# A wider look-ahead rule for the evacuating engine, together with a new scheduling table

## The chip, the cores and the metric

The kernel runs on one core of a Trainium2 chip. The metric is the device time of one execution in microseconds (us). The span of a profile is some 2.3 us shorter than its device time.

## The reference

It is one transformer layer on 2048 tokens of width 1024 in bf16. There are 32 query heads of width 32, but only one key head and one value head. The gated feed-forward part has width 3584.

```python
q = (x @ wq) as 32 heads;  k = x @ wk;  v = x @ wv          # k, v: one head of 32
p = softmax(q k^T * 32**-0.5);  attn = (p @ v) @ wo
h  = x + A(layernorm(x))                                    # A is the attention above
h2 = h + B(layernorm(h)),  B(x) = (sigmoid(x@w_gate) * (x@w_up)) @ w_down
```

## The kernel before

The program is a list scheduler. While the kernel is built, it simulates the engines with a table of assumed durations. It decides step by step what TensorE does next, and it fixes for each engine the order of its instructions. The built program holds these fixed orders, and its engines wait for each other at semaphores.

The spine is 512 "score visits". A visit is one block of eight row-tiled score matmuls, followed by two exponentials on ScalarE (`Pr`, 128x1024 each). Everything else on TensorE is filler between the visits: query projections, keys and values, probabilities times values (PV), output projections, feed-forward groups. If nothing can run, the scheduler puts in a matmul on the identity whose result nobody uses, called a dummy here.

In this program a finished PSUM bank is copied out ("evacuated") by ScalarE or VectorE: the query projections of 256 columns (`QTb`) took 384 to 478 ns on ScalarE and 418 to 425 ns on VectorE in before. This function chooses which of them does it:

```python
def evac(fn_act, fn_dve, n, deps, prio, dve_rate=0.96):
    now = pl.free["pe"]
    ready = now + 300.0 if v < 2 else 1e9
    a = max(pl.free["act"], now) + sum(o.occ for o in pl.heap["act"] if o.ready <= ready) + n / 1.2
    d = max(pl.free["dve"], now) + sum(o.occ for o in pl.heap["dve"] if o.ready <= ready) + n / dve_rate
    if a + (1000.0 * KNOBS[v // WIN][3] if v else 0.0) < d:
        return pl.op("act", fn_act, deps, prio=prio, **t_act(n))
    return pl.op("dve", fn_dve, deps, prio=prio, **t_dve(n, dve_rate))
```

`v` is the current visit. In visits 0 and 1 only those waiting operations count as backlog whose inputs will be there within 300 ns. Later all of them count (`1e9`).

`KNOBS` has 65 rows of eight small integers, one row for each eight visits (`WIN = 8`). They set thresholds and priorities. Entry 3 is an extra charge on ScalarE in us.

```python
pl.ahead = 100.0 * KNOBS[v // WIN][0] if v else 400.0
...
if can_s and run - t < 250.0 + 250.0 * KNOBS[v // WIN][4]:   # issue the next score visit now?
...
for cl in PRIO[KNOBS[v // WIN][2]]:                           # which filler class first
```

The first four x tiles are transposed on TensorE. The rest are transposed by DMA on the sync engine's queue, which also carries the stores of q and the weight loads:

```python
xT_ev[t] = dma(lambda: SP.dma_start_transpose(out=xnT4[t // 4][...], in_=x_sb[:, t, :]),
               f"xT{t}", ..., [xnorm[t]], prio=0, occ=1330.0)
...
q_store.append(dma(lambda: SP.dma_start(q_dram[:, g, tok:tok + n], qst[:, s, 0:n]), f"qs{s}", ..., [ev], prio=2))
```

The softmax here doesn't subtract the row's maximum and nothing guards it: scores larger than these inputs give would overflow.

## Time and profile before

| | before |
|---|---|
| device time | 1080.02 us, median of 3 (1079.95 to 1080.45) |
| span of the profiled run | 1078.0 us |
| last exponential ends | 1015.90 us |
| score matmuls of visit 3 start | 22.48 us |
| dummies in the front / later | 14 / 22 |

### The profile page before, as it was taken

The numbers are of one execution on the slowest core, as the hardware profiler recorded it, in microseconds if no ns is written. First come the engines' busy times: TensorE is split into PE (matmuls) and PEld (weight loads), VectorE is DVE, ScalarE is ACT, GpSimd is POOL, SyncE is SP. The second block draws the span as 40 slices with busy tenths as digits, with TensorE's granted clock in tenths as the row PEclk, the third lists the DMA queues.
The fourth block names the chain that finished last, engine by engine and source line by source line (L and its number), as shares of the span: only waits on it lengthen the run. The fifth ranks groups of instructions, "written<-read, shape, count | busy, mean of one in ns | idle before, by whom it ended". The sixth has DMA issues, their size and how long they took to land.

```text
span 1078.0 us, 31453 instructions
## 1 busy us (share of the span) xinstructions
PE 1043.5 (97%) x12925; PEld 489.3 (45%) x13094; DVE 903.2 (84%) x1736; ACT 1009.8 (94%) x1167; POOL 30.6 (3%) x58
## 2 busy tenths in 40 slices
PE   8999999999999999999999999999999999999999
PEld 7764434444444444444444444444444444444445
DVE  7899999898989879898888989898887988888721
ACT  6999999999999999999999999999999999999700
POOL 2100000000000000000000000000000000000000
PEclk9999999999999999999999999999999999999999
DMA  7997898929679695959879594955969489896994
GB/s 222 183 293 249 209 290 237 280 70 286 164 210 240 153 262 125 267 141 253 198 187 261 138 267 113 285 161 157 265 164 276 109 232 199 208 234 161 294 277 106
DMA packets 308623, 227.14 MB, mean 211 GB/s; under 512 B 119808, under 2 KB 299904, under 8 KB 308480
## 3 DMA queue, kind: packets, MB, share of 16 engines
q1 hardware_dynamic: 307296, 224.92, 81.8%
q8 instruction: 103, 1.69, 0.7%
q14 instruction: 40, 0.33, 0.1%
q10 hardware_dynamic: 1184, 0.20, 0.1%
HBM read 195.17 MB, written 7.86 MB: 188 GB/s over the span
## 4 chain that ended last, share of the span: by engine, by line
PE 73%; ACT 19%; issue 4%; DVE 2%; DMA 1%; SPq 0%; DVEq 0%
PE F_ps L415 57%; ACT Pr L707 18%; PE S_ps L415 16%; ACT tnh L1009 1%; DVE Ts L741 1%; DMA ring<-in_B_w_up_dram 1%; DVE Rc L806 0%; DMA ring<-in_A_x_dram 0%; DVE st L346 0%; DVE Oc L796 0%; DVE hact L291 0%; DVE st L348 0%; PE F_ps L444 0%; DVE Oc L291 0%; DVE Ts L748 0%
## 5 line engine op out<-in xcount | busy, mean ns | idle before, releaser
L707 ACT ACTIVATE Pr<-S_ps 128x1024 bf16<-128x1024 f32 x1024 | 968.9, 1156 | 3.3 <-PE S_ps L415 2.6
L741 DVE TENSOR_TENSOR Ts<-Ts,Pr 128x1024 bf16<-128x1024 bf16 x736 | 481.5, 677 | 33.7 <-ACT Pr L707 31.4
L415 PE MATMUL F_ps<-ring,hnT 128*128 128x512 bf16 (+1 forms) x1870 | 400.7, 380 | 13.1 <-issue 8.5
L415 PEld LDWEIGHTS F_ps<-ring,hnT 128*128 128x128 bf16 (+1 forms) x1957 | 147.6, 97 | 189.5 <-issue 48.3
L415 PE MATMUL S_ps<-QTb,kT 32*128 32x256 bf16 x4096 | 206.2, 273 | 1.2
L415 PE MATMUL F_ps<-zone,hact 128*128 128x512 bf16 (+2 forms) x1106 | 197.5, 377 | 9.5 <-issue 9.0
L415 PEld LDWEIGHTS S_ps<-QTb,kT 32*128 32x128 bf16 x4096 | 63.1, 92 | 206.3 <-ACT Pr L707 153.4
L415 PE MATMUL F_ps<-Pr,Vb 128*32 128x256 bf16 x4064 | 134.2, 274 | 0.3 <-issue 0.3
L415 PEld LDWEIGHTS F_ps<-zone,hact 128*128 128x128 bf16 (+1 forms) x1164 | 75.0, 97 | 83.5 <-issue 23.0
L415 PEld LDWEIGHTS F_ps<-Pr,Vb 128*32 128x32 bf16 x4064 | 96.8, 96 | 29.9 <-issue 17.0
L741 DVE TENSOR_TENSOR Ts<-Pr 128x1024 bf16<-128x1024 bf16 x128 | 86.6, 684 | 25.6 <-ACT Pr L707 25.1
L1013 DVE SCALAR_TENSOR_TENSOR hst<-tnh,F_ps 128x512 bf16<-128x512 f32 x107 | 73.3, 685 | 38.3 <-PE F_ps L415 36.4
L1009 ACT ACTIVATE tnh<-F_ps 128x512 f32<-128x512 f32 x105 | 77.5, 738 | 5.7 <-PE F_ps L415 5.7
L415 PE MATMUL F_ps<-zone 128*128 128x256 bf16 (+4 forms) x658 | 72.2, 272 | 2.3 <-issue 1.1
L415 PE MATMUL F_ps<-wo_sb,OT 128*128 128x512 bf16 (+1 forms) x283 | 58.4, 380 | 1.7 <-issue 1.6
L415 PEld LDWEIGHTS F_ps<-zone 128*128 128x128 bf16 (+1 forms) x667 | 43.1, 97 | 22.8 <-issue 7.4
L748 DVE TENSOR_TENSOR Ts<-Ts 128x1024 bf16<-128x1024 bf16 x64 | 43.9, 686 | 1.1
L358 POOL TENSOR_SCALAR zb<-mvb 128x1 bf16<-128x1 bf16 (+1 forms) x25 | 9.9, 397 | 993.6 <-DVE mvb L350 993.6
L1009 ACT ACTIVATE tnh<-S_ps 128x512 f32<-128x512 f32 x7 | 4.2, 597 | 35.3 <-PE S_ps L415 35.3
L291 DVE COPY Oc<-F_ps 128x256 f32<-128x256 f32 x60 | 25.3, 422 | 11.6 <-PE F_ps L415 10.7
L415 PEld LDWEIGHTS F_ps<-wo_sb,OT 128*128 128x128 bf16 (+1 forms) x294 | 21.0, 97 | 26.2 <-issue 6.8
L796 DVE TENSOR_TENSOR Oc<-F_ps,Oc 128x256 f32<-128x256 f32 x59 | 24.9, 423 | 7.5 <-PE F_ps L415 6.4
(84 smaller groups left out, 415.4 us busy)
## 6 DMA issues: line engine op xcount, KB each, us to landing
ring<-in_B_w_gate_dram SPq DMA_DIRECT2D x318, 256.0 KB, 4.8
ring<-in_B_w_up_dram SPq DMA_DIRECT2D x316, 256.0 KB, 4.6
zone<-in_B_w_down_dram SPq DMA_DIRECT2D x28, 256.0 KB, 3.7
h_sb<-in_A_x_dram SPq DMA_DIRECT2D x16, 256.0 KB, 4.5
out_dram<-h_sb SPq DMA_DIRECT2D x31, 128.0 KB, 3.0
ring<-in_A_x_dram SPq DMA_DIRECT2D x7, 512.0 KB, 5.3
QTb<-q_scratch SPq DMA_DIRECT2D x14, 256.0 KB, 5.4
Pr<-in_B_w_gate_dram SPq DMA_DIRECT2D x10, 256.0 KB, 4.1
```

What stands on the lines that cost most here:

```text
L291: lambda: DVE.tensor_copy(out=out_ap, in_=in_ap))
L358: f = pl.op("pool", lambda: POOL.tensor_scalar(out=zb[:, ph, sl].unsqueeze(2), in0=mvb[:, ph, sl, 1:2], scalar1=LN_EPS_BF16, scalar2=None, ...
L415: fn = lambda: PE.matmul(o, lhsT=l, rhs=r, start=start, stop=stop, **kw)
L707: exps[u] = pl.op("act", lambda slot=slot, pb=pb: ACT.activation(out=pslot(slot).rearrange("p (a b) -> p a b", a=2), in_=S_ps[:, pb:pb + 2 ...
L741: o = pl.op("dve", lambda T=T, a=a, b=b: DVE.tensor_tensor(out=T, in0=a, in1=b, op=ALU.add), deps, prio=4, **t_dve(1024, 1.92))
L748: merge_ev[G] = pl.op("dve", lambda T4=T4: DVE.tensor_tensor(out=T4[:, :, 0, :], in0=T4[:, :, 0, :], in1=T4[:, :, 1, :], op=ALU.add), [sum ...
L796: a = pl.op("dve", lambda: DVE.tensor_tensor(out=Oc[:, :], in0=O, in1=Ob, op=ALU.add), [last, oc_ev[G], o_ev.get(G - 1)], prio=0, **t_dve( ...
L1009: tanh_of[n] = pl.op("act", lambda: ACT.activation(out=tnh[:, :], in_=FB(b), func=ACTF.Tanh, scale=0.5), [last, tn_user.get(0)] + (tn_more ...
L1013: e = pl.op("dve", lambda: DVE.scalar_tensor_tensor(out=hst[:, n % NST, :], in0=tnh[:, :], scalar=1.0, in1=FB(b), op0=ALU.add, op1=ALU.mul ...
```

## The change

Its intent is that during visits 2 and 3 too, an operation that can't start yet should not count as a backlog. VectorE, waiting for a tile of x, would then get evacuations that ScalarE had to do between its exponentials.

```diff
-    KNOBS = [(4, 7, 0, 2, 2, 0, 0, 0), (0, 4, 0, 4, 1, 0, 0, 0), (2, 5, 0, 1, 3, 2, 1, 0), ... 62 more rows cut
+    KNOBS = [(4, 7, 1, 1, 2, 0, 0, 0), (0, 4, 1, 0, 2, 1, 0, 0), (2, 6, 0, 1, 2, 1, 1, 1), ... 62 more rows cut
...
-            ready = now + 300.0 if v < 2 else 1e9
+            ready = now + 300.0 if v < 4 else 1e9
```

More of the change, by code (lines that the diff above doesn't have):

```diff
@@ L170, in bass_sequential_preLN__grouped_kv_mqa__glu_gated_glu__prompt_kernel @@
     NCR = 12
-    KNOBS = [(4, 7, 0, 2, 2, 0, 0, 0), (0, 4, 0, 4, 1, 0, 0, 0), (2, 5, 0, 1, 3, 2, 1, 0), (3, 4, 1, 2, 3, 1, 1, 0), (3, 4, 0, 4, 2, 2, 1, 0), (1, 5, 1, 2, 3, 0, 1, 0), (4, 4, 0, 2, 2, 1, 0, 0), (4, 4, 1, 1, 3, 1, 1, 0), (1, 0, 0, 4, 3, 2, 0, 0), (3, 0, 1, 4, 2, 2, 0, 0), (1, 4, 1, 2, 3, 0, 1, 0), (4, 5, 0, 4, 2, 2, 0, 0), (3, 7, 0, 1, 3, 0, 0, 0), (2, 0, 1, 4, 2, 1, 0, 0), (3, 4, 0, 2, 2, 0, 1, 0), (2, 4, 0, 0, 3, 0, 1, 0), (3, 0, 0, 4, 3, 2, 0, 0), (2, 0, 0, 2, 3, 0, 1, 0), (0, 5, 0, 1, 3, 0, 0, 0), (1, 7, 1, 0, 3, 1, 0, 0), (0, 7, 0, 0, 3, 0, 1, 0), (2, 7, 0, 1, 3, 0, 0, 1), (4, 7, 0, 1, 3, 1, 1, 0), (1, 0, 1, 1, 3, 0, 0, 1), (4, 4, 0, 1, 3, 0, 0, 0), (3, 4, 1, 2, 3, 0, 1, 0), (2, 7, 0, 0, 3, 0, 1, 1), (0, 4, 1, 2, 2, 1, 1, 0), (3, 7, 1, 1, 2, 0, 1, 1), (4, 5, 0, 4, 3, 0, 0, 0), (4, 6, 0, 4, 3, 0, 0, 0), (2, 6, 1, 0, 3, 1, 1, 0), (1, 5, 1, 1, 2, 0, 1, 0), (4, 0, 0, 0, 2, 0, 0, 0), (4, 0, 0, 2, 3, 0, 1, 0), (2, 4, 0, 2, 2, 0, 1, 0), (0, 4, 0, 0, 3, 0, 0, 0), (3, 5, 0, 1, 2, 2, 0, 1), (1, 4, 0, 2, 2, 1, 1, 1), (4, 0, 0, 0, 3, 1, 0, 1), (1, 0, 0, 2, 3, 0, 0, 0), (2, 7, 0, 1, 3, 1, 0, 0), (3, 0, 0, 1, 2, 0, 0, 1), (1, 4, 0, 0, 3, 1, 1, 1), (0, 0, 1, 4, 2, 0, 0, 1), (3, 7, 0, 4, 3, 0, 0, 0), (1, 5, 1, 1, 2, 2, 0, 0), (4, 4, 0, 4, 2, 1, 1, 0), (0, 4, 0, 4, 3, 0, 1, 0), (1, 7, 0, 0, 2, 0, 1, 0), (1, 6, 0, 0, 3, 2, 1, 1), (2, 7, 0, 1, 3, 1, 0, 0), (4, 6, 1, 4, 2, 0, 0, 0), (0, 4, 0, 0, 2, 0, 0, 0), (4, 0, 0, 4, 3, 2, 1, 0), (3, 5, 1, 1, 3, 1, 0, 0), (2, 7, 0, 0, 3, 0, 0, 0), (3, 0, 0, 4, 2, 0, 1, 0), (4, 5, 0, 0, 3, 1, 0, 0), (4, 6, 0, 4, 1, 2, 0, 0), (4, 0, 0, 4, 3, 0, 0, 0), (4, 4, 0, 2, 2, 2, 0, 0), (4, 5, 0, 1, 1, 0, 1, 0), (4, 5, 1, 2, 2, 0, 0, 0), (2, 0, 0, 0, 2, 0, 0, 0)]
@@ new lines, in bass_sequential_preLN__grouped_kv_mqa__glu_gated_glu__prompt_kernel @@
+    KNOBS = [(4, 7, 1, 1, 2, 0, 0, 0), (0, 4, 1, 0, 2, 1, 0, 0), (2, 6, 0, 1, 2, 1, 1, 1), (2, 6, 1, 2, 2, 0, 0, 1), (0, 5, 1, 1, 3, 2, 1, 0), (3, 7, 1, 2, 3, 1, 1, 0), (0, 4, 0, 2, 2, 1, 0, 0), (3, 4, 1, 0, 3, 1, 1, 0), (1, 0, 0, 4, 3, 0, 0, 1), (3, 0, 0, 4, 3, 2, 0, 1), (3, 7, 1, 0, 3, 1, 1, 0), (4, 4, 1, 4, 3, 1, 0, 1), (3, 0, 0, 1, 3, 0, 1, 1), (2, 0, 0, 2, 3, 0, 1, 0), (3, 4, 0, 4, 3, 0, 1, 0), (2, 4, 0, 0, 3, 0, 1, 0), (3, 4, 0, 4, 2, 2, 0, 0), (2, 0, 1, 2, 2, 0, 1, 0), (0, 5, 0, 1, 3, 0, 0, 0), (3, 0, 1, 4, 3, 1, 1, 0), (3, 4, 1, 0, 2, 1, 1, 0), (2, 0, 1, 2, 2, 0, 0, 0), (4, 7, 0, 0, 3, 1, 1, 0), (4, 4, 1, 0, 3, 0, 0, 1), (2, 4, 0, 2, 3, 0, 0, 1), (0, 4, 1, 2, 3, 0, 0, 0), (2, 7, 0, 2, 3, 0, 1, 1), (4, 0, 1, 1, 2, 1, 1, 0), (3, 7, 1, 1, 3, 0, 1, 1), (4, 5, 0, 4, 2, 2, 0, 0), (3, 6, 0, 4, 3, 0, 0, 1), (2, 5, 1, 2, 2, 1, 1, 0), (1, 5, 1, 1, 2, 0, 1, 0), (4, 0, 0, 2, 2, 0, 0, 0), (4, 0, 0, 1, 3, 0, 1, 0), (2, 4, 1, 1, 2, 0, 0, 1), (4, 6, 1, 2, 3, 0, 1, 0), (1, 5, 0, 2, 3, 0, 0, 1), (1, 7, 0, 2, 2, 1, 1, 1), (3, 0, 1, 1, 3, 2, 1, 1), (4, 0, 0, 2, 2, 1, 0, 0), (2, 4, 0, 1, 3, 0, 0, 0), (0, 0, 0, 1, 2, 0, 0, 0), (1, 4, 0, 0, 3, 1, 0, 1), (0, 0, 1, 4, 2, 0, 0, 1), (3, 7, 0, 4, 3, 0, 0, 0), (4, 0, 0, 0, 2, 1, 0, 1), (4, 4, 0, 4, 2, 1, 1, 0), (3, 4, 0, 4, 3, 0, 1, 1), (4, 7, 0, 2, 2, 0, 1, 0), (3, 0, 0, 0, 2, 0, 1, 1), (4, 7, 1, 1, 2, 2, 0, 0), (4, 6, 0, 4, 2, 0, 0, 0), (2, 5, 0, 0, 2, 0, 1, 0), (0, 6, 0, 4, 2, 0, 0, 1), (3, 5, 1, 1, 3, 1, 0, 0), (2, 7, 0, 0, 3, 0, 0, 0), (2, 0, 0, 4, 2, 0, 1, 0), (4, 4, 0, 0, 3, 0, 0, 0), (4, 5, 1, 1, 2, 0, 1, 1), (4, 5, 1, 2, 2, 0, 0, 0), (4, 4, 0, 2, 3, 2, 0, 0), (4, 5, 0, 1, 1, 0, 1, 0), (4, 5, 1, 2, 2, 0, 0, 0), (2, 0, 0, 0, 1, 0, 1, 0)]
```

## The prediction

Passages that no trace of this case shows are cut from the text. In rival (c) a cut term made the gain up to 4 us, which gave its 1076; without that term it is 1080.0 - 1.2 - 2.4 = 1076.4 us. The 384 and 413 to 425 ns are evacuations of 256 columns; on VectorE the shortest of that size in before took 369 ns (`kT`), and the two of `QTb` 418 and 425.

> **What bounds the kernel now.** I read the page first: how busy each engine is, then the chain that ended last.
>
> ```profile
> PE 1043.5 (97%) x12925; PEld 489.3 (45%) x13094; DVE 903.2 (84%) x1736; ACT 1009.8 (94%) x1167; POOL 30.6 (3%) x58
> PE 73%; ACT 19%; issue 4%; DVE 2%; DMA 1%; SPq 0%; DVEq 0%
> ```
>
> Two engines look full: TensorE at 97% and ScalarE at 94%. The chain runs 73% of the span through TensorE and 19% through ScalarE. To see which of them sets the end, I cut the span into stretches. The columns are stretch, length, busy time of PE, PEld, DVE, ACT and POOL, granted clock, DMA share and GB/s.
>
> ```profile
> 10.00:20.00 10.00, 8.69 (x155) 7.35 (x153) 8.28 (x21) 7.99 (x15) 1.17 (x3) 1.00 0.91 309
> 20.00:30.00 10.00, 9.21 (x136) 7.03 (x134) 9.21 (x28) 9.28 (x16) 2.59 (x6) 1.00 0.68 127
> 30.00:40.00 10.00, 10.00 (x166) 7.36 (x167) 9.85 (x30) 8.87 (x15) 2.14 (x4) 1.00 0.86 199
> 600.00:700.00 100.00, 97.43 (x1233) 43.63 (x1247) 87.85 (x165) 99.97 (x116) 2.19 (x3) 1.00 0.82 208
> 700.00:800.00 100.00, 97.78 (x1208) 43.34 (x1213) 87.02 (x165) 100.00 (x115) 2.33 (x4) 1.00 0.68 177
> 800.00:900.00 100.00, 96.59 (x1207) 43.49 (x1225) 86.24 (x162) 100.00 (x117) 1.49 (x2) 1.00 0.86 220
> 1030.00:1050.00 20.00, 19.89 (x92) 9.09 (x93) 3.16 (x5) 1.79 (x3) 0.00 (x0) 1.00 1.03 275
> ```
>
> From about 60 to 1000 us ScalarE has no gap (the exponentials) and TensorE has 2 to 3.5 us of gap in each 100. After the last exponential, which the timeline puts at 1015.9, ScalarE is nearly idle (1.79 of 20 us) and TensorE alone works off the rest of the feed-forward part, about 60 us. So the last word is TensorE's. What it hasn't done beside the exponentials, it does after them. Its work is the same before and after the change, hence **end = TensorE's fixed work + what it loses to waits and dummy matmuls**. A microsecond that TensorE gains anywhere is a microsecond at the end, as long as there is other matmul work to fill in. From 30 us on there is: 10.00 of 10 busy.
>
> The change acts in score visits 2 and 3, from the score matmuls of visit 1 (14.49 us in the timeline) to those of visit 3 (22.48). There I read the chain in order of time: start, length, what.
>
> ```profile
> 13.28 2.85 ACT Pr L707 x3
> 16.13 0.28 ACT QTb L290
> 16.41 0.49 ACT zone L290
> 16.90 0.93 ACT Pr L707
> 17.82 0.05 issue
> 17.87 0.68 PE S_ps L415 x9
> 18.55 0.22 PE F_ps L444 x4
> 18.77 0.28 PE S_ps L415 x5
> ...
> 21.09 1.02 ACT Pr L707
> 22.11 0.28 ACT kT L290
> 22.39 0.92 ACT Pr L707
> 23.30 0.28 ACT QTb L290
> ```
>
> Here ScalarE is on the chain, and between its exponentials (Pr) stand PSUM evacuations (L290: QTb, zone, kT). The 9 and 5 matmuls on S_ps are dummies on the identity, issued because nothing real could run. The two engines that may evacuate, in the timeline of the same stretch:
>
> ```profile
> 16.27 0.63 ACT L290 ACTIVATE zone<-F_ps 128x512 bf16<-128x512 bf16 x1
> 17.65 1.75 ACT L290 ACTIVATE zone<-F_ps 128x512 bf16<-128x512 bf16 x3
> 16.45 0.69 DVE L346 BATCH_NORM_STATS2 st<-ring 128x6 f32<-128x512 bf16 x1 [1.55 <-DMA ring<-in_A_x_dram]
> ```
>
> VectorE sat idle 1.55 us until 16.45, waiting for a tile of x, while ScalarE was given every evacuation from 16.0 to 23.7 us: QTb 3, zone 4, kT 1 and Vb 1, nine in all, 4.20 us of listed time (0.40 + 0.63 + 1.75 + 0.38 + 0.38 + 0.40 + 0.26). That is the fault that the edit aims at: the chooser counted VectorE's normalization work as a backlog though its input wasn't there.
>
> [...] weight loads are busy 45% where matmuls are 97%. But in the tail a run of 26 matmuls of 512 columns takes 5.61 us (chain of waits, at 1027.12), 216 ns each, so TensorE is streaming there. [...] at 1008.88 the weight loads stop and the row-tiled score loads begin at 1009.30, 0.42 us later, against the 0.216 us of one matmul. [...] the trace has 384 (ScalarE, undisturbed minimum) and 413 to 425 (VectorE). So a moved evacuation costs nearly the same; only the queue in front of it differs.
>
> **The change part by part.** No arithmetic, transfer or matmul is added or removed; only order and engines change.
>
> (1) The edit of the rule. In the stretch from 14.49 to 24 us TensorE's losses are: 0.69 us until QTb at 16.46, 0.52 us until the exponential at 17.87, about 0.96 us of dummies (0.68 + 0.28 on the chain), and 0.76 us until QTb at 23.63. Sum 2.93 us; that is the most that it can give. Not all of it: once the x tiles 4 and 5 have come at 16.45, VectorE's statistics are truly ready, some 0.6 us each with four or more in the queue, so the chooser will again go to ScalarE. I expect 3 or 4 of the nine to move, chiefly those before 17 us. Moving QTb and the first zone from before the fourth exponential brings this forward by 0.28 + 0.49 = 0.77 us on the chain, and the next transposes don't wait for it. I put the gain at 0.77 plus about half of the 0.96 of dummies: **1.2 us**. On the other side, each moved 512-column copy takes VectorE at most 0.69 us (the 512-column cast to hact on L291 shows 684 ns). Three or four moved copies of 0.4 to 0.7 are about 2 us, of which the idle 1.55 takes most; about 0.5 us is left that delays the normalization of later tiles, and VectorE is 92 to 98% busy from 20 to 40 us. I take nothing off for it, since TensorE has projections as filler there.
>
> (2) The table. 55 of its 65 rows differ. The row of the first eight visits lowers the extra charge on ScalarE from 2 to 1 us, which goes against (1). The second row lowers it from 4 to 0, so in visits 8 to 15 (about 31 to 48 us) evacuations go back to ScalarE, which has gaps of 0.25 to 0.57 us there. Past about 65 us this entry is dead and the rest are priorities and thresholds: they shuffle which filler runs when. What a shuffle can move, I read off the stretches: TensorE's gap in the eight stretches of 100 us from 200 to 1000 is 2.73, 2.73, 3.00, 2.88, 2.57, 2.22, 3.41 and 2.71 us, a standard deviation of 0.33. Drawn anew for ten such stretches that gives 0.33 x 3.2 = 1.0 us. The later dummies, 22 on kT and ident of 256 columns, at about 0.11 us (half of the 216 ns) come to 2.4 us, and the waits for weights of w_up to 3.4 + 1.3 us; a luckier table might save a third of this 7.1, 2.4 us, an unlucky one add as much. A table is kept because it came out well somewhere, and may be overfitted to the plan's own durations, so I expect **0.8 us** from it.
>
> Sum: 1080.0 - 1.2 - 0.8 = **1078.0 us**.
>
> **The rivals.** (a) VectorE becomes the brake. It is 9.21 and 9.85 of 10 us busy from 20 to 40 us, and it makes the x tiles whose keys later visits need. If evacuations push it back by the full 2 us, later visits come late, and the early gain is given back as dummies between 25 and 50 us. For: VectorE's load. Against: ScalarE's gaps there are small and TensorE shows 10.00 with no wait on normalization. Time then: 1079.5 to 1081. (b) Nothing is gained at the front because the ScalarE charge falls from 2 to 1 us and cancels the filter; then only the table's luck is left: 1080 +- 1.5. (c) The new table is a real find, removing later dummies and weight waits, for 2.4 us on top of 1.2[...]: 1076. For: 22 dummies and 4.7 us of waits for w_up are there to be had. Against: the gaps per 100 us are so alike that they look structural.
>
> **Range and chances.** The shuffle's spread of 1.0, the front's uncertainty of about 1 (from 0 to 2.9) and half of the 2.4 for dummies and weights add in squares to about 1.9; times 1.3 for 8 in 10 is 2.5. Leaning a little to gain: 1075.2 to 1080.8. A 2% change is 21.6 us, ten times the spread, so within 2% is nearly sure: 0.985, faster 0.01, slower 0.005.
>
> **What would show it.** Right: between 14.5 and 24 us three or four evacuations stand on VectorE (L291, QTb or zone), its idle 1.55 us is partly filled, the 14 dummies shrink to under 8, the score matmuls of visit 3, now at 22.48, come 1 us or more earlier, and so does the exponential stream; TensorE's gaps from 200 to 1000 us stay at 2 to 3.5 us per 100. Wrong: the visits aren't earlier though evacuations moved (rival a, with VectorE or KV waits after them); the same engines evacuate (rival b); or the front is earlier but the last exponential, now at 1015.9, isn't; or the gaps or w_up waits in the middle change by more than the front does (rival c, or its opposite).

## More of the kernel before

The profiled run is one of the timed runs, except for before, whose profile is of one more run (1080.3 us).

## The result

| | before, same rounds | after |
|---|---|---|
| device time, median of 6 | 1079.97 (1079.75 to 1080.45) | 1080.65 (1080.02 to 1081.62) |
| ratio, 95% interval | | 1.0006 (0.9994 to 1.0019): same |
| span of the profiled run | 1078.0 | 1078.1 |
| score matmuls of visit 3 start | 22.48 | 21.39 |
| last exponential ends | 1015.90 | 1017.24 |
| dummies in the front / later | 14 / 22 | 10 / 10 |

The page of the profile after, first engine busy times, then the chain's shares by engine:

```profile
PE 1042.1 (97%) x12849; PEld 489.1 (45%) x13021; DVE 901.0 (84%) x1733; ACT 1008.9 (94%) x1170; POOL 30.5 (3%) x58
PE 77%; ACT 14%; DVE 4%; issue 3%; DMA 2%; SPq 0%; POOL 0%; DVEq 0%; POOLq 0%
```

Nothing in it looks different except that the chain goes less through ScalarE (14% against 19%) and more through TensorE (77% against 73%). The stretches of after have the columns that the prediction explains, with 50 to 60 us added (most of the middle is left out):

```profile
10.00:20.00 10.00, 9.39 (x163) 7.66 (x160) 8.98 (x24) 7.00 (x13) 0.96 (x2) 1.00 0.90 307
20.00:30.00 10.00, 9.06 (x131) 6.92 (x130) 10.00 (x29) 9.82 (x17) 2.79 (x6) 1.00 0.73 136
30.00:40.00 10.00, 9.94 (x135) 7.25 (x136) 9.86 (x30) 8.29 (x16) 1.85 (x4) 1.00 0.88 202
50.00:60.00 10.00, 8.78 (x160) 6.24 (x161) 4.21 (x10) 8.62 (x11) 0.00 (x0) 1.00 0.97 325
700.00:800.00 100.00, 96.67 (x1205) 43.10 (x1223) 88.49 (x169) 100.00 (x115) 2.96 (x4) 1.00 0.75 188
1030.00:1050.00 20.00, 19.56 (x90) 8.76 (x91) 3.14 (x5) 1.79 (x3) 0.00 (x0) 1.00 1.07 293
```

The first row is better: TensorE is busy 9.39 of 10 us instead of 8.69. But between 50 and 60 us TensorE now has a hole of 1.22 us. In before that stretch was full:

```profile
50.00:60.00 10.00, 10.00 (x167) 6.83 (x155) 5.93 (x14) 9.75 (x12) 0.00 (x0) 1.00 0.96 296
```

The front works as intended. In the timeline of VectorE after, these three copies, the L291 lines, stood on ScalarE before:

```profile
15.49 0.42 DVE L291 CAST QTb<-F_ps 128x256 bf16<-128x256 f32 x1 [0.68 <-PE F_ps L415]
15.83 0.41 DVE L291 COPY zone<-F_ps 128x512 bf16<-128x512 bf16 x1
16.41 0.42 DVE L291 COPY zone<-F_ps 128x512 bf16<-128x512 bf16 x1 [0.16 <-PE F_ps L444]
```

The chain of after, in order of time, shows what that does. ScalarE has only its four exponentials there, and the first run of dummies is 5 instead of 9:

```profile
13.18 3.78 ACT Pr L707 x4
16.96 0.05 issue
17.00 0.45 PE S_ps L415 x5
17.46 0.22 PE F_ps L444 x4
17.68 0.28 PE S_ps L415 x5
```

The score matmuls of visit 3 follow. The first line is from the timeline of before, the second from that of after:

```profile
22.48 0.40 PE L415 MATMUL S_ps<-QTb,kT 32*128 32x256 bf16 x8
```

```profile
21.39 0.40 PE L415 MATMUL S_ps<-QTb,kT 32*128 32x256 bf16 x8
```

So the gain is real at 21 us and gone at 1078. To see where it goes I kept an account. From the program I took the order of TensorE's matmuls and gave each useful one the time that the plan's own table has for it: 216 ns for 512 columns (the traces show the same), nearly in proportion for fewer (the traces show 109 ns for 256 and 56 for 128), and about 0.1 us for each change of tiling (the traces show 0.096 us: a score block starts 0.312 us after the last 512-column matmul ahead of it, median of 361 cases in before, where the next such matmul would start after 0.216). For each visit I subtracted the time of all useful work ahead of it from the moment at which its score matmuls start in the trace. What is left is TensorE's lost time up to there: waits and dummies. The useful work is the same in both kernels (1051.05 and 1051.12 us), so the columns can be compared. This is my computation from the traces, not a view of the profile. The last column belongs to the last experiment below.

| lost by TensorE, us | before | after | last experiment |
|---|---|---|---|
| start to visit 5 | 12.25 | 11.16 | 10.94 |
| visits 5 to 14 (about 25 to 50 us) | 0.43 | 1.56 | 1.56 |
| visit 14 to 15 (about 50 to 52 us) | 0.01 | 1.37 | 0.00 |
| visits 15 to 384 | 6.81 | 6.75 | 6.09 |
| visits 384 to 392 (about 764 to 780 us) | 2.20 | 0.36 | 0.35 |
| visits 392 to 511 | 2.80 | 2.74 | 2.79 |
| sum at visit 511 | 24.50 | 23.94 | 21.73 |
| span of the run | 1078.03 | 1078.05 | 1076.01 |

The front gains 1.09 us. Then 1.13 us is lost again by visit 14 and 1.36 us at visit 15. Far later 1.84 us comes back, and after the last visit another 0.58 us is lost (the span grows by 0.02 though the sum falls by 0.56). Added up: -1.09 + 1.13 + 1.36 - 0.06 - 1.84 - 0.06 + 0.58 = +0.02 us. The account is of the two profiled runs, which took 1080.3 and 1080.35 us. The medians differ by 0.68 us, so a typical run of after loses some 0.6 us more than the account shows.

The lines behind three of these rows are in TensorE's timeline. In after there are new dummies at 29 and 37 us, and a wait for a transposed tile of x (`zone<-ring`) until 51.67:

```profile
29.27 0.45 PE L415 MATMUL S_ps<-ident 128*128 128x128 bf16 x5
36.80 0.45 PE L415 MATMUL S_ps<-ident 128*128 128x128 bf16 x5
51.67 0.92 PE L415 MATMUL F_ps<-zone 128*128 128x256 bf16 x7 [1.22 <-DMA zone<-ring]
```

In before, 16 of the 22 later dummies stand here, and after has none of this kind:

```profile
769.82 0.94 PE L415 MATMUL F_ps<-kT,ident 128*128 128x256 bf16 x7
771.05 1.16 PE L415 MATMUL F_ps<-kT,ident 128*128 128x256 bf16 x9
```

Why does TensorE wait for x at 50 us only in after? In before it does two visits' PV blocks just there. These are the first lines of the two:

```profile
46.78 1.06 PE L415 MATMUL F_ps<-Pr,Vb 128*32 128x256 bf16 x32
48.97 1.06 PE L415 MATMUL F_ps<-Pr,Vb 128*32 128x256 bf16 x32
```

In after it has done the same kind of work seven microseconds earlier, and needs the last x tiles sooner. The transposes themselves do not come later: the last one is issued at 46.93 us in after and at 48.51 in before. That the earlier need is the reason is read from these lines and was not tested by moving the PV blocks:

```profile
39.90 1.06 PE L415 MATMUL F_ps<-Pr,Vb 128*32 128x256 bf16 x32
42.09 1.06 PE L415 MATMUL F_ps<-Pr,Vb 128*32 128x256 bf16 x32
```

### The profile page after: what moved, and what is told of

Read it like the earlier page. It is cut to its first block, busy times and chain, and to the rows that moved or that the text cites. A ratio compares the mean times of both kernels' runs of the same rounds, so it can differ in the third digit from the quotient of the medians.

```text
span 1078.1 us, 31329 instructions
## 1 busy us (share of the span) xinstructions
PE 1042.1 (97%) x12849; PEld 489.1 (45%) x13021; DVE 901.0 (84%) x1733; ACT 1008.9 (94%) x1170; POOL 30.5 (3%) x58
## 4 chain that ended last, share of the span: by engine, by line
PE 77%; ACT 14%; DVE 4%; issue 3%; DMA 2%; SPq 0%; POOL 0%; DVEq 0%; POOLq 0%
PE F_ps L415 61%; PE S_ps L415 16%; ACT Pr L707 12%; DVE Ts L741 2%; ACT tnh L1009 1%; DMA ring<-in_B_w_up_dram 1%; DMA hnT<-hn 0%; DMA zone<-ring 0%; DMA hact<-hst 0%; DMA ring<-in_A_x_dram 0%; DVE Rc L806 0%; DVE hact L291 0%; DVE st L348 0%; DVE hst L1013 0%; DVE Oc L291 0%
## 5 line engine op out<-in xcount | busy, mean ns | idle before, releaser
L707 ACT ACTIVATE Pr<-S_ps 128x1024 bf16<-128x1024 f32 x1024 | 970.4, 1170 | 4.7 <-PE S_ps L415 4.5
L415 PE MATMUL F_ps<-zone,hact 128*128 128x512 bf16 (+1 forms) x1060 | 192.8, 380 | 9.9 <-issue 9.5
L415 PEld LDWEIGHTS F_ps<-zone,hact 128*128 128x128 bf16 (+1 forms) x1121 | 72.0, 97 | 83.8 <-issue 24.4
L415 PE MATMUL F_ps<-zone 128*128 128x256 bf16 (+5 forms) x655 | 72.6, 271 | 3.4 <-DMA zone<-ring 1.2
L291 DVE COPY Oc<-F_ps 128x256 f32<-128x256 f32 x60 | 25.3, 422 | 14.1 <-PE F_ps L415 13.4
```

The costliest lines, as they stand in the source:

```text
L291: lambda: DVE.tensor_copy(out=out_ap, in_=in_ap))
L415: fn = lambda: PE.matmul(o, lhsT=l, rhs=r, start=start, stop=stop, **kw)
L707: exps[u] = pl.op("act", lambda slot=slot, pb=pb: ACT.activation(out=pslot(slot).rearrange("p (a b) -> p a b", a=2), in_=S_ps[:, pb:pb + 2 ...
```

## The experiments

The working theories were these. **Order:** the new table leads to another order, and this order has waits of its own at fixed places. Whatever TensorE loses there is lost at the end. **VectorE:** the moved copies hold up the normalization of x, so the front gain itself is given back (the prediction's first rival). **ScalarE:** evacuations left on ScalarE between 25 and 37 us hold the banks. **Chance:** differences of 1 us are luck of when transfers land. Letters in the texts are those texts' own.

Building the kernel anew replans everything. To change one thing, I let the program plan as before and moved single operations only afterwards, in the finished lists of each engine. I call such a kernel frozen. All of them use this hook, in which `rearrange` is what each experiment fills in:

```diff
-                return pl.op("act", fn_act, deps, prio=prio, **t_act(n))
-            return pl.op("dve", fn_dve, deps, prio=prio, **t_dve(n, dve_rate))
+                return keep(pl.op("act", fn_act, deps, prio=prio, **t_act(n)), act=fn_act, dve=fn_dve)
+            return keep(pl.op("dve", fn_dve, deps, prio=prio, **t_dve(n, dve_rate)), act=fn_act, dve=fn_dve)
...
-        lists = pl.lists
+        lists = pl.lists; rearrange(lists, exps, mm)
```

`keep` numbers the evacuations in `EV`. `move(lists, k, eng, at)` takes evacuation `k` to an engine, behind the operation `at`. Lines that only name a list (`pe`, `sp`) are left out of the cuts. All twelve kernels gave the right result. Times are medians.

### 1. Only the three moved evacuations, in the order of before (three_moved)

```diff
+    move(lists, 7, "dve", EV[4])
+    move(lists, 6, "dve", EV[4])
+    move(lists, 5, "dve", EV[4])
+    for o in [o for o in lists["pe"] if o.tag == "dummy" and exps[3] in o.deps][:4]:
+        lists["pe"].remove(o)
```

> The schedule of the kernel before, frozen as it was planned, with one thing changed: the three evacuations that the changed kernel moved (one QTb, two zone, between 15 and 17 us) stand on VectorE, and 4 of the 9 dummies that had waited for them are gone. Both theories: the score matmuls of visit 3 come at about 21.4 us instead of 22.48. Theory A (TensorE's fixed work decides, a gain at the front is a gain at the end): 1.1 us less at the end, about 1078.9. Theory B (the gain is absorbed before 55 us, because TensorE runs ahead of the tiles of x, whose normalization on VectorE and whose transposes set their own pace): the first exponential of visit 6 (31.71 before) is early by less than 0.3 us, or late, and the end is within 0.4 us of before.

Measured: 1078.89 us (runs 1080.78, 1078.89, 1079.44, 1078.82, 1078.87) against 1079.78, ratio 0.9993 (0.9979 to 1.0006). Visit 3 starts at 21.48. Four of five runs are 0.3 to 1.0 us below before. The profiled one is the exception, and its timeline of TensorE says why:

```profile
44.73 0.81 PE L415 MATMUL F_ps<-zone 128*128 128x256 bf16 x6 [1.83 <-DMA zone<-ring]
```

This is the same kind of wait as in after, for a transposed tile, and before has none there. The edit of the front alone is worth about 0.9 us at the end in the undisturbed runs, close to the gain at visit 3, with an interval that still touches 1.

### 2. The three evacuations put back, in the order of after (three_back)

```diff
+    move(lists, 6, "act", exps[2])
+    move(lists, 5, "act", exps[2])
+    move(lists, 7, "act", exps[3])
```

> The schedule of the changed kernel, frozen, with the three evacuations put back on ScalarE in the old places. Both: visit 3's score matmuls at about 22.4 us instead of 21.39. Theory A: 1.1 us more at the end than the changed kernel, about 1081.7. Theory B: the lost microsecond is taken out of the dummies near 29 us and of the 1.2 us that TensorE sits idle at 50.5 to 51.7 us, and the end stays within 0.4 us of the changed kernel, about 1080.6.

Measured: 1080.93 us against 1079.78, ratio 1.0012 (0.9999 to 1.0024). By my account it has lost 0.97 us more than after at visit 5 and still 0.71 us more at visit 511, so most of the front's gain survives to the last visit in these two profiles. The device times don't decide between the two texts: 1080.93 is 0.28 us above after's 1080.65, as Theory B had it, and 1.13 above the 1079.8 of after_again, as Theory A had it. It loses 1.45 us between visits 5 and 8, and so does after (11.16 to 12.62). Therefore this loss is not caused by the moved copies. The VectorE theory falls.

### 3. Ten more matmuls in the middle, in the order of before (mid_pad)

```diff
+    pad(10, "GU", 100)      # ten 512-column matmuls ahead of the 100th gate/up group
```

> The schedule of the kernel before, frozen, with ten extra matmuls of 512 columns (10 x 216 ns = 2.16 us) put ahead of one gate/up group in the middle of the run, far from the front; the result stays right. Theory that TensorE's work decides: the end is 2.2 us later, about 1082.2 (ratio 1.002). Rival, that ScalarE sets the pace in the middle and TensorE has slack there: less than 0.5 us.

Measured: 1081.86 us against 1079.78, ratio 1.0021 (1.0007 to 1.0035). Added work of 10 x 0.216 = 2.16 us costs 2.08 us. TensorE's lost time in the middle of the kernel does come out at the end, although in before ScalarE has no gap there. (In mid_pad ScalarE is busy 98.19 of the 100 us from 500 on, in before 100.00: it can be made to wait.)

### 4. The loads of wo later, in the order of after (late_wo)

```diff
+    late = [o for o in sp if o.key.startswith("wo")]      # 8 loads, now behind the store that followed them
+    store = [o for o in sp[sp.index(late[0]):] if o.key.startswith("qs")][0]
+    for o in late:
+        sp.remove(o)
+        sp.insert(sp.index(store) + 1 + late.index(o), o)
```

> The schedule of the changed kernel, frozen, with the eight loads of wo issued behind the store at 52.4 us instead of right behind the last two transposes of x at 48.4. If the 1.2 us idle of TensorE at 50.5 comes from these loads slowing the transposes (which landed at 51.5): the idle shrinks by 0.5 us or more. If it comes from VectorE having normalized the last tiles no sooner: it stays at 1.1 to 1.3 us. In the end time: up to 1.2 us less under theory A, within 0.4 under theory B.

Measured: 1080.67 us (runs 1079.26, 1080.9, 1079.63, 1080.94, 1080.67) against 1079.78, ratio 1.0005 (0.9992 to 1.0017). In the profiled run the loss at visit 15 is 0.81 instead of 1.37 us. The times fall into two bunches. The profile speaks against the loads: the last transpose landed 4.76 us after its issue (46.17 to 50.93), though the loads now came after it had landed, and 4.60 us after in the first profile of after (46.93 to 51.53). The wait was shorter because this run issued the transpose 0.76 us sooner; why it did is open.

### 5. After, once more (after_again)

> The changed kernel itself, unedited, so that the variants of it have their comparison on the same chip in the same rounds. 1080.3 to 1081.0 us, ratio 1.0006; the waits of TensorE at 29 and 50 us as in its first profile if they belong to the schedule, gone or moved if they were chance.

Measured: 1079.8 us (runs 1079.53, 1081.31, 1081.67, 1079.8, 1079.62) against 1079.93, ratio 1.0003 (0.9991 to 1.0016). The same waits are in its profile at 29 and 50 us: 1.23 us is lost at visit 15. One later wait of 0.75 us, at visits 288 to 296 of the first profile, is not. The median lies below the 1080.3 to 1081.0 that was expected. So the two big losses belong to the order, and chance adds or takes about a microsecond elsewhere.

### 6. Three moved and two transposes earlier, in the order of before (moved_hoist)

```diff
 (as three_moved, and)
+    i = [o.key for o in sp].index("xT10")
+    sp.insert(i + 1, sp.pop(i - 1))       # one store of q goes behind the transposes of x tiles 10 and 11
```

> The frozen schedule of before with the three evacuations on VectorE (as in three_moved), and besides the transposes of x tiles 10 and 11 issued ahead of one q store that held them up. If the late run of three_moved (1080.8, its profile with 1.83 us of waiting for a transpose at 44.7) came from the smaller margin of these transposes: all runs lie at 1078.6 to 1079.3, about 0.9 us below before. If not: again a run or two at 1080 or more.

Measured: 1079.15 us (1078.83 to 1079.22 in five runs) against 1079.93, ratio 0.9991 (0.9978 to 1.0005). The five times lie within 0.4 us and there is no late run. The expectation was met. It fits the view that the late run of three_moved came from this wait, but one late run in five against none in five can also be chance.

### 7. Four more evacuations on VectorE, in the order of after (evac_spread)

```diff
+    for k in (17, 18, 22, 24):            # evacuations to hact at 25 to 37 us
+        move(lists, k, "dve", slot(k))    # behind the last VectorE operation planned to end before k's input is there
```

> The frozen schedule of the changed kernel, with four evacuations of projections (hact, visits 6 to 8) moved from ScalarE to VectorE. Theory C (the new table gives the front gain back because, with the charge on ScalarE down from 2 to 1 and 0 us, the evacuations queue behind exponentials and TensorE waits for PSUM banks): the first exponential of visit 6, 32.14 in the changed kernel, comes 0.5 us or more earlier, and the end is 0.5 to 1.3 us earlier. Theory B (TensorE waits for the tiles of x): visit 6 is no earlier, rather later[...], and the end is the same or later.

Measured: 1080.91 us against 1079.93, ratio 1.0007 (0.9994 to 1.0019). Visit 6 comes 0.3 us earlier than in after (31.39 against 31.69), less than Theory C asked for. The loss from visit 5 to 6 falls from 0.84 to 0.56 us, but visits 7 to 8 lose 1.1 us instead, and the x tiles come later. The load is only moved between two busy engines: in the two stretches from 20 to 40 us of after VectorE is busy 10.00 and 9.86 of 10 us, ScalarE 9.82 and 8.29. At the 0.42 us that such a cast of 256 columns takes on VectorE in after, four come to 1.7 us, as an estimate. The waits are for ScalarE's evacuations, but moving them this way gains nothing.

### 8 and 9. The two halves of the change, planned anew (rule_only, table_only)

```diff
 rule_only                                             table_only
-    ready = now + 300.0 if v < 2 else 1e9             -    KNOBS = [old]
+    ready = now + 300.0 if v < 4 else 1e9             +    KNOBS = [new]
```

> The old table with the new rule (v < 4), planned anew. If table entries are nearly independent shuffles, as the prediction took them (spread 1.0 us): 1077.8 to 1080 us. If a table only fits the one sequence that it was found with: slower by 5 us or more, since every later choice falls at another place; the kernel's own plan says 10 us.

> The new table with the old rule (v < 2), planned anew. If a table only fits the sequence that it was found with, as rule_only (1088.0) has it: slower than before by 5 us or more. If the new table is good in itself and only the rule of the old one is needed for the old: 1079 to 1082.

Measured: rule_only takes 1087.95 us against 1079.93, ratio 1.0072 (1.0058 to 1.0086). table_only takes 1096.03 us against 1079.92, ratio 1.0148 (1.0132 to 1.0163). Each half alone is slower by 8 and by 16 us, and together they are even. The front gain is the rule's: visit 3 starts at 21.37 in rule_only and at 22.63 in table_only. Lines of table_only show what a table does on a sequence that it was not made for. The first is from the groups by line, the second from the chain near the end, the other two from TensorE's timeline there:

```profile
L415 PE MATMUL F_ps<-kT,ident 128*128 128x256 bf16 x63 | 8.2, 273 | 0.0
```

```profile
1038.52 5.00 DMA Pr<-in_B_w_up_dram
```

```profile
1039.04 2.24 PE L415 MATMUL F_ps<-kT,ident 128*128 128x256 bf16 x19
1043.57 0.61 PE L415 MATMUL S_ps<-Pr,hnT 128*128 128x512 bf16 x2 [0.58 <-DMA Pr<-in_B_w_up_dram]
```

It has 63 such dummies instead of the 22 of before. Thirty of them stand in the tail, where only TensorE works, around a weight load that takes 5 us to land. TensorE is not idle for these 5 us: it runs 30 dummies (30 x 0.108 = 3.2 us, an estimate with half of the 216 ns; in before such dummies start 0.109 us apart) and useful matmuls, and waits for the load 0.26 and 0.58 us, some 4 us lost in all. In these two runs a row of the table is fitted to one sequence of decisions and has no worth of its own.

### 10. After without its ten later dummies (no_dummy)

```diff
+    for o in [o for o in pe if o.tag == "dummy"][-10:]:
+        pe.remove(o)
```

> The frozen schedule of the changed kernel without its ten dummies in visits 6 and 8 (29.3 and 36.8 us), which the plan had put in as it held the keys of x tiles 4 to 7 not yet landed. Theory D (the dummies and nothing else take the time; the chip's data is there earlier than planned): the score matmuls of visit 8, 37.19 in the changed kernel, come 0.5 to 0.6 us earlier. Theory B (they only fill a wait for the transposes): visit 8 within 0.15 us of 37.19, and TensorE shows the wait in their place, on the DMA of zone from ring. In the end time at most 0.6 us, if the later transposes don't take it.

Measured: 1080.29 us against 1079.92, ratio 1.0004 (0.9992 to 1.0017). The loss from visit 5 to 6 stays 0.84 us. Visit 8 starts at 36.96 us, 0.23 earlier than in the first profile of after and 0.13 earlier than in the second: nearer to Theory B than to D. But the wait is not the one that Theory B named. In the place of the dummies, the weight loads now wait for the evacuation:

```profile
29.43 1.93 PEld L415 LDWEIGHTS F_ps<-zone 128*128 128x128 bf16 x31 [0.42 <-ACT hact L290]
```

### 11. The best version so far without the 22 later dummies of before (hoist_nodummy)

```diff
 (as moved_hoist, and)
+    for o in [o for o in pe if o.tag == "dummy"][-22:]:
+        pe.remove(o)
```

> moved_hoist (1079.15), and besides without the 22 dummies on kT and ident at 404 and 764 to 772 us. If the weights had come earlier than planned there, TensorE gains up to 22 x 0.108 = 2.4 us: about 1076.8. If the dummies filled a true wait for weights or banks: no gain, 1079.0 to 1079.2, with waits on the DMA of the ring in their place.

Measured: 1080.11 us (runs 1081.3, 1080.11, 1079.26, 1080.45, 1079.19) against 1079.92, ratio 1.0002 (0.9989 to 1.0014). Nothing is gained. TensorE waits for an exponential, not for the ring, where the dummies stood:

```profile
770.34 0.39 PE L415 MATMUL S_ps<-QTb,kT 32*128 32x256 bf16 x6 [0.62 <-ACT Pr L707]
```

The runs are of two kinds. The two with a mean granted clock of 1.0 took 1079.19 and 1079.26 us, as moved_hoist did (1079.15). The three with 0.998 took 1080.11 to 1081.3. The profiled run is one of these, and its stretches show where the clock fell. The first line is moved_hoist, the second this kernel; the granted clock is the number before the last two:

```profile
770.00:780.00 10.00, 9.79 (x112) 4.40 (x113) 9.51 (x19) 10.00 (x12) 0.00 (x0) 1.00 1.12 298
```

```profile
770.00:780.00 10.00, 9.03 (x96) 3.48 (x97) 8.60 (x17) 9.13 (x11) 0.00 (x0) 0.83 0.96 262
```

The two kernels differ in the 22 dummies alone. So at a full clock removing them changed nothing. In three of five runs the clock fell and 0.9 to 2.1 us were lost; in the profiled one it fell just behind the place of 16 of the dummies. That the missing dummies are the cause is not shown: every other run had a mean clock of 1.0, the five of no_dummy without its ten dummies among them.

In neither experiment did removing dummies gain time. The wait behind a dummy is the cost: 0.42 and 0.62 us of waiting stand in the two places shown.

### 12. After with its last transposes earlier (after_hoist)

The queue of the sync engine in after explains the wait at 51.67. This is its timeline, where a row is a run of issues:

```profile
39.80 1.54 SPq L597 DMA_DIRECT2D q_scratch<-hact  x3
41.38 3.60 SPq L470 DMA_TRANSPOSE zone<-ring  x2
45.02 0.58 SPq L597 DMA_DIRECT2D q_scratch<-hact  x1
45.65 2.61 SPq L470 DMA_TRANSPOSE zone<-ring  x2
```

One transpose of a tile (128x1024) holds this queue for 1.24 to 2.32 us (median of the twelve in after 1.32), and four stores of q stand between the last ones. From issue to landing a transpose took a median of 3.5 us in before and 4.4 us in after. The last one was followed in the chain by its landing, 4.6 us later:

```profile
46.93 4.60 DMA zone<-ring
```

The edit puts these four stores behind the last transpose and changes nothing else:

```diff
+    last = [o for o in sp if o.key.startswith("xT")][-1]
+    late = ...                            # the stores between the last five transposes
+    for o in late:
+        sp.remove(o)
+        sp.insert(sp.index(last) + 1 + late.index(o), o)
```

> The kernel after with its plan frozen; on the sync engine's queue the four stores of q that stand between the transposes of the last x tiles are put behind the last transpose (the issue of these stores takes 1.5 and 0.6 us, 39.80 to 41.34 and 45.02 to 45.60, in the profile of after). Everything else keeps its order. In after TensorE waits 1.22 us at 50.5 to 51.7 for these transposes. Theory (this wait is one of the places where the early gain is given back, and TensorE's loss there is a loss at the end): the last transposes are issued about 2 us sooner, the wait goes to under 0.3 us, the score matmuls of visit 15 come about 1 us earlier than in after, and the time falls by 0.7 to 1.2 us, to 1079.0 to 1079.6 if after stands at its 1080.2, with fewer runs above 1081. Rival (the wait stands where TensorE would lose the time anyway, because ScalarE or the next visits fill up): the wait shrinks, but the same time is lost within the next 50 us and the median stays at 1080 to 1081. Rival 2: the delayed stores hold the evacuation buffers and new waits appear for the evacuations at 40 to 48 us: 1081 or more.

Measured: **1078.3 us** (runs 1078.3, 1077.42, 1078.18, 1078.34, 1078.42) against 1079.76 (nine runs, 1079.57 to 1080.27), ratio 0.9983 (0.9970 to 0.9997). By the 2% yardstick this is "same", but the interval lies below 1. It is the fastest kernel, and all its runs are below every run of before and of after. It fell below the 1079.0 to 1079.6 that was expected for it. The queue's timeline and TensorE's stretch now read:

```profile
37.58 9.03 SPq L470 DMA_TRANSPOSE zone<-ring  x6
46.66 2.07 SPq L597 DMA_DIRECT2D q_scratch<-hact  x4
```

```profile
50.00:60.00 10.00, 10.00 (x175) 7.36 (x172) 5.81 (x13) 9.89 (x12) 0.00 (x0) 1.00 0.91 301
```

The chain runs through 50 us without a transfer:

```profile
49.14 0.33 PE S_ps L415 x8
49.47 1.53 PE F_ps L415 x13
50.99 0.33 PE S_ps L415 x8
```

The hole of 1.22 us is closed (10.00 of 10 instead of 8.78). In the account, the loss at visit 15 goes from 1.37 to 0.00, and the lead over the second profile of after is 1.42 us from visit 15 on and 1.64 us at visit 511 (23.37 against 21.73). The rival with the held buffers made no wait that the profile shows. The Order theory is confirmed for this place. It is about half of what ate the gain: 1.36 us, beside 1.13 between visits 5 and 14, in the first profile of after, and 1.22 beside 1.19 in the second.

## Why the prediction was right or wrong

"Within 2%" and the range were right. The time of 1078.0 was 2.65 us below the 1080.65 measured, which is close to the upper end of the range, so the margin hid an error of sign in one step. There was luck in it too: the working gives 2.5 us to either side and says that it leans to gain, but the range reaches 2.8 up and down. With 2.5 its upper end would have been 1080.5.

- **"End = TensorE's fixed work + what it loses"** held. mid_pad added 2.16 us of work and got 2.08. after_hoist removed one wait of about 1.4 us and its span is 2.0 us shorter than that of the first profile of after; 0.66 of it lies in visits 15 to 384, where after's own two profiles also differ.
- **Part 1, the rule, 1.2 us:** right in mechanism, a little too large. Three evacuations moved (3 or 4 foreseen). Visit 3 starts 1.09 us sooner. Of this, 0.10 is there at visit 1 already (14.39 against 14.49), 0.76 is the earlier end of the fourth exponential (0.77 foreseen), and 0.23 the dummies (0.96 to 0.73 us on the chain; 0.48 foreseen). The dummies of the front fell to 10, not under 8. A moved 512-column copy took 0.41 to 0.42 us on VectorE, not 0.69 (in before such copies took 0.59 to 0.67 us on ScalarE). The prediction had taken the duration of a cast from f32 (a median of 684 ns for 512 columns to `hact`) for a copy from bf16.
- **Part 2, the table, 0.8 us: this step failed.** The prediction treated the new table as one draw from equally good shuffles, with a small gain because it had been chosen. The account puts all that isn't the front at +1.13 + 1.36 - 0.06 - 1.84 - 0.06 + 0.58 = +1.11 us, a loss. In the second profile of after (span 1077.26) the front gains 1.19 us and the rest loses 0.42, so the sign holds and the size does not. The prediction had seen that the new table sends evacuations back to ScalarE in visits 8 to 15 and put no cost on it. From 25 to 48 us ScalarE does 14 evacuations in after and 9 in before, and TensorE's weight loads wait for them there (for `hact` on ScalarE 1.3 us in four waits in after, 0.5 us in two in before); which part of the loss this is stays open (evac_spread). The rule and the table are one object: apart they cost 8 and 16 us. Against rule_only the new table gains some 7 us: what it bought was mainly the repair of a plan that the rule had upset. One benefit is real, the vanished hole at 764 to 772 us (1.84 us), near the 2.4 us that the prediction had named for all later dummies.
- **The spread of 1.0 us for a shuffle, from TensorE's gaps per 100 us,** rests on an artefact. Those gaps of 2 to 3.5 us are largely matmul records missing from the trace: three_moved, which has the order of before there, shows 100.00 of 100 where before shows 97.27.

```profile
200.00:300.00 100.00, 97.27 (x1252) 43.35 (x1272) 88.68 (x170) 100.00 (x115) 2.97 (x4) 1.00 0.74 183
```

```profile
200.00:300.00 100.00, 100.00 (x1267) 43.46 (x1266) 88.76 (x169) 100.00 (x115) 2.97 (x4) 1.00 0.75 186
```

The first line is before and has 1252 matmuls for 1272 weight loads. The second is three_moved and has 1267 for 1266.

- **The change of tiling** was read too large. The prediction set the 0.42 us without weight loads at 1008.88 against 0.216; the profile puts this pause down to the wait for an exponential (`<-ACT Pr L707`). A change of tiling costs 0.096 us by the starts of the matmuls (0.312 less 0.216). With some two changes a visit that is about a tenth of the run, as an estimate from these figures.

- **Rival (a)** foresaw the right time (1079.5 to 1081) and nearly the right place ("given back as dummies between 25 and 50 us"; 1.36 us of it came just after 50, and as a wait), but by the wrong mechanism. three_back, with the copies off VectorE again, loses the same 1.45 us between visits 5 and 8. **Rival (b)** did not happen, as three evacuations moved. **Rival (c)** happened in half: the later dummies of before are gone and the waits for w_up shrank (from 3.4 + 1.3 to 1.4 + 0.6 us), but the new order paid for it elsewhere.
- **"The front is earlier but the last exponential isn't"** was listed as a sign of being wrong, and it is what the trace shows (the last one ends at 1017.24 against 1015.90).

What stays open: the 1.13 us between visits 5 and 14. The weight loads wait there for evacuations on ScalarE, the dummies only fill those waits (no_dummy), and moving evacuations to VectorE shifts the wait (evac_spread). Which part of the order would have to change is not shown. Nor did I test the 0.58 us after the last visit, or the earlier PV blocks as the reason for the wait at 50 us.

## What to carry to other kernels

In this static schedule a rule and its tuned table could not be judged by halves, and the same may hold for others. Plan once, freeze the order, and move single operations in it to learn what one of them is worth. Keep an account of the bounding engine's lost time along the program: it showed a gain of 1.1 us being spent within 30 us, about half of it on a wait for a transfer that stood behind stores nobody was waiting for yet. When such a wait is found, look at what stands ahead of it in the issuing queue before touching the engines. A dummy marked a wait in both experiments on it, and removing it left the wait (0.42 and 0.62 us); in one of the two it also came with a lower clock in three of five runs.
